# Half-height chunk transfers, weight decoding one pair sooner and two sums on GpSimd in the attention stage of a fused attention and feed-forward kernel

## The chip, the cores and the metric

One core of a Trainium2 chip runs the whole program. The metric is the time of one execution on the device in microseconds (us), the median of three runs. A profiled execution of the same program, with its own time, is the source of every row below.

The engines of the core are named as in the profile: PE is TensorE's matmul side and PEld its weight loads, DVE is VectorE, ACT is ScalarE, POOL is GpSimd, and SP is SyncE, which here only issues transfers (its queue is SPq).

## The reference

Three blocks run one after the other: a decayed linear attention over 768 tokens, 4 batches and 8 heads of 64 features, and then two feed-forward blocks over the 3072 tokens.

```python
state = zeros((B, H, D, D))
for t in range(S):
    state = gamma * state + einsum('bhd,bhe->bhde', k[:, :, t], v[:, :, t])
    y[:, :, t] = scale * einsum('bhd,bhde->bhe', q[:, :, t], state)
x = y.transpose(0, 2, 1, 3).reshape(B * S, H * D)
h = (x @ w1) * (x @ w2) @ w3          # d_ff = 1024
x = h @ w_out
h = maximum(maximum(x @ v1, x @ v2), x @ v3)   # d_ff = 768
y = h @ v_out
```

## The kernel before

**The attention stage.** The tokens of each batch are cut into chunks of 128, six to a batch, 24 in all (`CPB`, `NCH`). `seq` lists them in the order of work: batches 0 and 1 take turns for twelve chunks, then batches 2 and 3. The loop steps over pairs, `i` and `i + 1`. For a chunk the kernel computes scores (`scores`, L360), multiplies them by a mask on DVE (`attn_mask`, L365), scales v on POOL (`scale_v`, L350, with the decay factors that `decays` copies on DVE, L343), multiplies q with the running state (`attn_in`, L373), multiplies the masked scores with v (`attn_av`, L382), updates the state (`attn_st`, L393, copied by ACT, L395) and moves the result out of PSUM with its output factors on DVE (`attn_ev`, L400). Scores, masks and scaled v of the next pair are made at the end of a pair (`scores_ahead`); in the pair that ends the first two batches (`turn`, i = 10) they are made in its middle. The order of the instructions on every engine is the order of this code.

**The chunks' transfers.** A chunk is a tile of 128 partitions with four rows of 512 numbers in each: q, k, the key by token and v. `load_half` (L327) brings two of the rows, q and k or the other two, 4 KB for each partition and 512 KB in all (256 KB where a batch's last chunk needs v alone). Six chunk tiles stand in a ring (`NCK`). At the end of pair `i` the SP queue gets the four transfers of chunks `i + 6` and `i + 7`, and in the first six pairs one transfer of weights after them (`early`, L93 inside `fetch`); two more go out ahead of the loop.

**Decoding the weights.** The weights arrive as 64-bit numbers. A unit is 512 KB of them, and eight units are decoded during the attention stage. `step` alternates `decode_a` and `decode_b`. Taking in a unit (`decode_front`) is an absolute value on ACT (L124) and a clip on POOL (L126); then follow two instructions on DVE (L147, L149), a conversion on ACT (L156) and an addition on DVE (L141). `decode_b` already takes in the following unit on ACT and POOL. `plan` says at which place of which pair a step or another job is put: place 1 lies between `attn_in` and `attn_av` of the pair's first chunk, place 2 behind that chunk, and place 3 behind `scores_ahead`.

**The operands of the first feed-forward block.** Its products are formed with seven multiplications of sums in place of eight, each operand held as a high and a low part. `wgen.parts(q)` splits a weight operand into the two parts, on ACT (L211) and DVE (L212); `wgen.sums` forms sums of the raw weights on DVE (L216, L218 to L220), with `tmp`, which is `s_t`, as a buffer. `op_split` does the splitting for the activations (L254, L255), and `op_first` forms their first difference (L266). The first matmuls (L573 to L575) need the parts of operand and weight 0; the next groups need those of 1, of 2, and so on. Some of these jobs stand in `plan`, and the rest between the attention stage and the first matmul group, from L533 on, in the code's order.

Of the kernel before, what the change touches and what calls it, by code (L numbers as in the profile page):

```python
# [12 lines left out]
ALU = mybir.AluOpType  # L13
ACT = mybir.ActivationFunctionType

P = 128
# [3 lines left out]
CPB = S // C  # L20
# [27 lines left out]
def fused_kernel(ctx: ExitStack, tc: tile.TileContext, ck, w12, w3t, wo1, w123, wo2, mask, gout, gch, kdec, out):  # L48
    nc = tc.nc
# [15 lines left out]
    def spill(n, q):  # L65
        return opsp[n, q].rearrange("h p x -> p h x")

    def halves(t):
        return t.bitcast(F32).rearrange("p (h x) -> p h x", h=2)
# [135 lines left out]
    def weights(raw, n, slot=wslot, tmp=None):  # L205
        tmp = s_t[:, :n] if tmp is None else tmp
        r0, r1, r2, r3 = raw

        def parts(q):
            src, w = (r0, r1, r0, r2, tmp, r3, r1)[q], slot(q, n)  # L210
            nc.scalar.copy(out=w[:, 0], in_=src)  # L211
            nc.vector.tensor_tensor(out=w[:, 1], in0=src, in1=w[:, 0], op=ALU.subtract)  # L212

        def sums(q):
            if q == 0:
                return [lambda: nc.vector.tensor_tensor(out=tmp, in0=r2, in1=r3, op=ALU.add)]  # L216
            if q == 1:
                return [lambda: nc.vector.tensor_tensor(out=r2, in0=r2, in1=r0, op=ALU.subtract),  # L218
                        lambda: nc.vector.tensor_tensor(out=r0, in0=tmp, in1=r0, op=ALU.subtract),
                        lambda: nc.vector.tensor_tensor(out=r1, in0=r1, in1=r0, op=ALU.subtract)]  # L220
            return []

        def emit(q):
            for job in jobs(q):
                job()

        def jobs(q):
            return [lambda: parts(q)] + sums(q)

        emit.jobs, emit.parts, emit.sums = jobs, parts, sums  # L230
        return emit

    def raw_quads(n):
        return [wraw_t[0][:, i * n:(i + 1) * n] for i in range(4)]
# [14 lines left out]
    def view2(t):  # L249
        return t.rearrange("p (k n) -> p k n", k=2)  # L250

    def split_to(o, src):
        o = o.rearrange("p (h k n) -> p h k n", h=2, k=2)
        nc.scalar.copy(out=o[:, 0], in_=src)  # L254
        nc.vector.tensor_tensor(out=o[:, 1], in0=src, in1=o[:, 0], op=ALU.subtract)  # L255

    def op_split(s, src):
        split_to(op_t[s % 4][:, :], src)
# [3 lines left out]
    def t_buf(n):  # L262
        return view2(work["T"][:, :1024])

    def op_first(quad):
        nc.vector.tensor_tensor(out=quad(0, 0), in0=quad(0, 1), in1=quad(0, 0), op=ALU.subtract)  # L266

    def op_pre(n, q, quad, quiet=False):
        t, sub = t_buf(n), ALU.subtract
        if q == 2:  # L270
            op_first(quad)
            nc.vector.tensor_tensor(out=t, in0=quad(1, 1), in1=quad(0, 0), op=sub)
        elif q == 3:
            eng = nc.vector if quiet else nc.gpsimd
            eng.tensor_tensor(out=quad(0, 1), in0=quad(1, 1), in1=quad(0, 1), op=sub)
        elif q == 5:
            nc.vector.tensor_tensor(out=t, in0=t, in1=quad(1, 0), op=sub)
# [33 lines left out]
    def half(hh):  # L311
        return slice(64 * hh, 64 * hh + 64)

    seq = [(2 * g + z, j) for g in range(2) for j in range(CPB) for z in range(2)]
    last = len(seq) - 1

# [3 lines left out]
    def cks(i):  # L320
        return ck_t[i % NCK]

    def load_half(i, z):
        if i <= last:
            b, j = seq[i]
            o = 3 if z and j == CPB - 1 else 2 * z
            nc.sync.dma_start(out=cks(i)[:, o:2 * z + 2, :], in_=ck[b * CPB + j, :, o:2 * z + 2, :])  # L327

    def bank4(k, n=NP):
        return bank[k].rearrange("p (n c) -> p n c", n=n)  # L330
# [81 lines left out]
    def quad_b(n):  # L412
        return lambda k, e: xr_t[n][:, 2 * k:2 * k + 2, e, :]
# [4 lines left out]

    with tc.manual_schedule():
        load_half(0, 0)  # L420
        nc.scalar.dma_start(out=kdec_sb, in_=kdec)
        load_half(1, 0)
        nc.scalar.dma_start(out=mask_sb, in_=mask)
        load_half(0, 1)
        load_half(1, 1)
        nc.vector.memset(warm_sb, 0.0)
# [20 lines left out]
        for i in range(2):  # L447
            scores(i)
            attn_mask(i)
        wgen = weights(raw_quads(1024), 1024)  # L450
        ops_b = {}
        plan = {
            (4, 1): [step],
            (4, 3): [step],
            (6, 1): [step],
# [1 line left out]
            (8, 1): [step],  # L457
            (8, 3): [step],
            (10, 1): [step],
            (10, 3): [step],  # L460
            (12, 1): [step],
            (12, 2): [lambda: wgen.parts(0)],
            (12, 3): [step],
            (14, 1): [step],
            (14, 2): [lambda: op_split(0, quad_b(0)(0, 0))],
            (14, 3): [step],
            (16, 1): [step],
            (16, 2): [lambda: wgen.parts(1)],
            (16, 3): [step],
            (18, 1): [step],  # L470
            (18, 2): [lambda: op_first(quad_b(0))],
            (18, 3): [step],
            (20, 1): [step],
            (20, 2): [wgen.sums(0)[0]],
            (20, 3): [wgen.sums(1)[0]],
        }

        def place(i, z):
# [52 lines left out]
        rwa = b_pl.tile([P, 2048], F32, name="rwa")  # L531
        b_pl.tile([P, 24], F32, name="pad_b")
        op_split(1, quad_b(0)(1, 0))  # L533
        wgen.sums(1)[1]()
        wgen.parts(2)
        nc.vector.tensor_tensor(out=t_buf(0), in0=quad_b(0)(1, 1), in1=quad_b(0)(0, 0), op=ALU.subtract)
        op_split(2, t_buf(0))
        for t in range(3):
            nc.sync.dma_start(out=spill(0, t), in_=halves(op_t[t]))
        op_pre(0, 3, quad_b(0), quiet=True)  # L540
# [9 lines left out]
        wgen = weights(raw_quads(1024), 1024)  # L550
        for g in range(KF // GA):
            for n in range(NB):
                blk = g * NB + n
                sets = sets_b(blk)
                for q in range(7):
# [13 lines left out]
                    for p in range(GA):  # L569
# [32 lines left out]
                        z = p if blk > NB else 2 * q + p // 2  # L602
# [3 lines left out]
                    z = s - 7 * (NB - 1) - LAG  # L606
# [118 lines left out]
        wgen = weights(raw_quads(256 * GH), 256 * GH)  # L725
        GEN = (15, 18, 21, 24, 27, 30, 33, 36)
        XL = 0
        for s in range(XS):
            n, r = divmod(s, 14)
            q, kk = divmod(r, 2)  # L730
# [10 lines left out]
            for m in range(2):  # L741
                ps = bank[(4 if n % 2 == 0 else 0) + (2 if which == "b" else 0) + m]
                o = slice(m * P, (m + 1) * P)
# [77 lines left out]
        for j in range(GH):  # L821
# [14 lines left out]
            wgen = weights(raw_quads(256 * GH), 256 * GH)  # L836
# [91 lines left out]
        for s in range(7 * NB):  # L928
            n, q = divmod(s, 7)
# [9 lines left out]
            for r in range(2):  # L939
                ps = o_sets[n % 2][which][r]  # L940
                o = slice(r * P, (r + 1) * P)
# [87 lines left out]
```

## Time and profile before

| | |
|---|---|
| median of three runs | 819.75 us (819.7 to 819.98) |
| the profiled execution: time | 818.71 us |
| the profiled execution: span from first to last instruction | 816.4 us |
| outside the span | 2.31 us |
| busy: PE, DVE, ACT, POOL | 805.8, 631.4, 388.2, 74.6 us |
| granted clock of TensorE | 0.999 |
| first matmul of the feed-forward block | 82.8 us after the start |

The span runs from the first instruction to the last. The attention stage fills its first tenth. Busy time of an engine says how long it worked, not that its work decided the end; which wait ends last is read from the chain of waits and from the timeline.

### The profile page before, as it was taken

Reading aid. Unit: us, or ns where it says so; the run is one execution under the profiler, and the core shown is the slowest. Engines: PE = TensorE matmul, PEld = TensorE weight load, DVE = VectorE, ACT = ScalarE, POOL = GpSimd, SP = SyncE. Lnnn points to the kernel's source line nnn. Section 1 sums busy time; section 2 is a strip of 40 time slices with the busy share of each in tenths; the row PEclk is TensorE's granted clock in tenths of the full one; section 3 lists DMA queues with packets and bytes.
Section 4 is the critical chain, followed back from the end, with each engine's and each line's share of the span. In section 5 each row is a group of like instructions: output and inputs, shape, how many; then the busy total and the mean of one; then the engine's idle time right before and its main releaser. Section 6 shows DMA issues by size and latency. Waiting matters only on the chain.

```text
span 816.4 us, 12177 instructions
## 1 busy us (share of the span) xinstructions
PE 805.8 (99%) x4648; PEld 672.6 (82%) x4648; DVE 631.4 (77%) x795; ACT 388.2 (48%) x589; POOL 74.6 (9%) x93
## 2 busy tenths in 40 slices
PE   8999999999999999999999999999999999999998
PEld 8888888888888888888888888888888888888886
DVE  3799898989598988779799839994565565688793
ACT  2442545463336454557577545453334334434642
POOL 2443000000011111001010000000000000000000
PEclk9999999999999999999999999999999999999999
DMA  9997598789999984686789798989998699956522
GB/s 346 406 408 309 212 363 342 294 336 327 371 334 416 361 327 181 217 305 214 266 300 364 260 345 308 365 297 406 409 324 304 239 336 352 321 214 216 205 104 78
DMA packets 69961, 246.55 MB, mean 302 GB/s; under 512 B 6416, under 2 KB 6544, under 8 KB 69904
## 3 DMA queue, kind: packets, MB, share of 16 engines
q1 hardware_dynamic: 48672, 165.97, 53.8%
q10 hardware_dynamic: 21232, 79.81, 27.2%
q8 instruction: 37, 0.61, 0.3%
q14 instruction: 20, 0.16, 0.0%
HBM read 163.97 MB, written 81.79 MB: 301 GB/s over the span
## 4 chain that ended last, share of the span: by engine, by line
PE 93%; DVE 0%; issue 0%; ACT 0%; ACTq 0%
PE bank L872 11%; PE bank L873 10%; PE bank L874 10%; PE bank L575 9%; PE bank L574 9%; PE bank L573 9%; PE bank L746 5%; PE bank L747 5%; PE bank L748 5%; PE bank L944 4%; PE bank L945 4%; PE bank L943 3%; PE bank L662 2%; PE bank L661 2%; PE bank L663 2%; PE abank L382 1%
## 5 line engine op out<-in xcount | busy, mean ns | idle before, releaser
L573 PE MATMUL bank<-op,w 128*128 128x512 f32 x336 | 130.8, 389 | 0.0
L575 PE MATMUL bank<-op,w 128*128 128x512 f32 x336 | 130.7, 389 | 0.0
L574 PE MATMUL bank<-op,w 128*128 128x512 f32 x336 | 130.7, 389 | 0.0
L872 PE MATMUL bank<-op,w 128*128 128x512 f32 x330 | 128.5, 389 | 0.0
L874 PE MATMUL bank<-op,w 128*128 128x512 f32 x330 | 128.4, 389 | 0.0
L873 PE MATMUL bank<-op,w 128*128 128x512 f32 x330 | 128.4, 389 | 0.0
L126 POOL TENSOR_SCALAR dec<-dec 128x512 f32<-128x512 f32 x64 | 46.6, 729 | 554.4 <-ACT dec L124 520.5
L573 PEld LDWEIGHTS bank<-op,w 128*128 128x128 f32 x336 | 63.1, 188 | 13.3 <-issue 0.2
L574 PEld LDWEIGHTS bank<-op,w 128*128 128x128 f32 x336 | 63.1, 188 | 13.2
L575 PEld LDWEIGHTS bank<-op,w 128*128 128x128 f32 x336 | 63.1, 188 | 12.9
L872 PEld LDWEIGHTS bank<-op,w 128*128 128x128 f32 x330 | 61.9, 188 | 13.5 <-ACT bank L877 0.5
L874 PEld LDWEIGHTS bank<-op,w 128*128 128x128 f32 x330 | 61.9, 188 | 13.0
L873 PEld LDWEIGHTS bank<-op,w 128*128 128x128 f32 x330 | 61.9, 188 | 12.6
L748 PE MATMUL bank<-op,w 128*128 128x512 f32 x168 | 65.4, 389 | 0.0
L746 PE MATMUL bank<-op,w 128*128 128x512 f32 x168 | 65.4, 389 | 0.0
L747 PE MATMUL bank<-op,w 128*128 128x512 f32 x168 | 65.4, 389 | 0.0
L156 ACT ACTIVATE dec<-stg 128x512 int32<-128x512 uint32 x49 | 33.1, 676 | 52.2 <-DVE stg L149 45.8
L147 DVE TENSOR_SCALAR dec<-dec 128x512 int32<-128x512 int32 x64 | 27.0, 422 | 22.7 <-POOL dec L126 22.7
L124 ACT ACTIVATE dec<-stg 128x512 f32<-128x512 f32 x49 | 32.6, 664 | 12.7 <-DMA stg<-in_w_dram 6.5
L885 DVE TENSOR_TENSOR m<-m,bank 128x512 f32<-128x512 f32 x34 | 23.3, 684 | 19.5 <-PE bank L874 18.9
L944 PE MATMUL bank<-w,wo 128*128 128x512 f32 x96 | 37.4, 390 | 0.0
L945 PE MATMUL bank<-w,wo 128*128 128x512 f32 x96 | 37.4, 389 | 0.0
(216 smaller groups left out, 1581.7 us busy)
## 6 DMA issues: line engine op xcount, KB each, us to landing
op<-opsp ACTq DMA_DIRECT2D x53, 1024.0 KB, 8.1
opsp<-op SPq DMA_DIRECT2D x34, 1024.0 KB, 5.7
ck<-in_ck_dram SPq DMA_DIRECT2D x44, 512.0 KB, 10.1
fsp<-C SPq DMA_DIRECT2D x24, 512.0 KB, 4.8
op<-opsp SPq DMA_DIRECT2D x10, 1024.0 KB, 6.0
hsp<-m SPq DMA_DIRECT2D x32, 256.0 KB, 6.0
stg<-in_w_dram SPq DMA_DIRECT2D x15, 512.0 KB, 9.3
U<-fsp SPq DMA_DIRECT2D x14, 512.0 KB, 5.9
```

Of the source, the lines that this page charges most:

```text
L126: nc.gpsimd.tensor_scalar(out=df, in0=df, scalar1=MAX_HI, scalar2=MIN_HI, op0=ALU.min, op1=ALU.max)
L573: nc.tensor.matmul(ps, wh, x[:, 0, k, :], start=first and k == 0 and not seeded, stop=False, skip_group_check=True)
L574: nc.tensor.matmul(ps, wh, x[:, 1, k, :], start=False, stop=False, skip_group_check=True)
L575: nc.tensor.matmul(ps, wl, x[:, 0, k, :], start=False, stop=k == 1, skip_group_check=True)
L746: nc.tensor.matmul(ps, wh, x[:, 0, k, :], start=first and kk == 0 and k == 0, stop=False, skip_group_check=True)
L747: nc.tensor.matmul(ps, wh, x[:, 1, k, :], start=False, stop=False, skip_group_check=True)
L748: nc.tensor.matmul(ps, wl, x[:, 0, k, :], start=False, stop=kk == 1 and k == 1, skip_group_check=True)
L872: nc.tensor.matmul(ps, wh, x[:, 0, k, :], start=first and k == 0 and not seeded, stop=False, skip_group_check=True)
L873: nc.tensor.matmul(ps, wh, x[:, 1, k, :], start=False, stop=False, skip_group_check=True)
L874: nc.tensor.matmul(ps, wl, x[:, 0, k, :], start=False, stop=k == 1, skip_group_check=True)
L944: nc.tensor.matmul(ps, wh[:, k, o], xl[:, k], start=False, stop=False, skip_group_check=True)
L945: nc.tensor.matmul(ps, wl[:, k, o], xh[:, k], start=False, stop=k == 2, skip_group_check=True)
```

## The change

From the nineteenth chunk on (`i >= HALVES`, 18) each transfer of `load_half` becomes two, one for partitions 0 to 63 and one for 64 to 127. The decode steps begin in pair 2 in place of pair 4 and keep their order; the same 17 steps are placed, so that the last one stands in pair 18. `parts(0)` moves from pair 12 to pair 10, `parts(1)` from pair 16 to pair 18. `op_first` and the first of the weight sums go to GpSimd, at the end of pairs 16 and 18. The second sum stands in the middle of pair 20, the third one, until now behind the loop, in pair 22. Behind the loop `parts(2)` is placed after the second activation split.

```diff
-        def sums(q):
+        def sums(q, eng=nc.vector):
             if q == 0:
-                return [lambda: nc.vector.tensor_tensor(out=tmp, in0=r2, in1=r3, op=ALU.add)]
+                return [lambda: eng.tensor_tensor(out=tmp, in0=r2, in1=r3, op=ALU.add)]
...
-    def op_first(quad):
-        nc.vector.tensor_tensor(out=quad(0, 0), in0=quad(0, 1), in1=quad(0, 0), op=ALU.subtract)
+    def op_first(quad, eng=nc.vector):
+        eng.tensor_tensor(out=quad(0, 0), in0=quad(0, 1), in1=quad(0, 0), op=ALU.subtract)
...
+    HALVES = 18
...
-            nc.sync.dma_start(out=cks(i)[:, o:2 * z + 2, :], in_=ck[b * CPB + j, :, o:2 * z + 2, :])
+            n = P if i < HALVES else P // 2
+            for r in range(0, P, n):
+                nc.sync.dma_start(out=cks(i)[r:r + n, o:2 * z + 2, :], in_=ck[b * CPB + j, r:r + n, o:2 * z + 2, :])
...
         plan = {
+            (2, 1): [step],
+            (2, 3): [step],
             (4, 1): [step],
...
             (10, 1): [step],
+            (10, 2): [lambda: wgen.parts(0)],
             (10, 3): [step],
             (12, 1): [step],
-            (12, 2): [lambda: wgen.parts(0)],
             (12, 3): [step],
             (14, 1): [step],
             (14, 2): [lambda: op_split(0, quad_b(0)(0, 0))],
             (14, 3): [step],
             (16, 1): [step],
-            (16, 2): [lambda: wgen.parts(1)],
-            (16, 3): [step],
+            (16, 3): [step, lambda: op_first(quad_b(0), nc.gpsimd)],
             (18, 1): [step],
-            (18, 2): [lambda: op_first(quad_b(0))],
-            (18, 3): [step],
-            (20, 1): [step],
-            (20, 2): [wgen.sums(0)[0]],
-            (20, 3): [wgen.sums(1)[0]],
+            (18, 2): [lambda: wgen.parts(1)],
+            (18, 3): [lambda: wgen.sums(0, nc.gpsimd)[0]()],
+            (20, 2): [wgen.sums(1)[0]],
+            (22, 1): [wgen.sums(1)[1]],
         }
...
         op_split(1, quad_b(0)(1, 0))
-        wgen.sums(1)[1]()
-        wgen.parts(2)
         nc.vector.tensor_tensor(out=t_buf(0), in0=quad_b(0)(1, 1), in1=quad_b(0)(0, 0), op=ALU.subtract)
         op_split(2, t_buf(0))
+        wgen.parts(2)
```

## Rows read from the trace of the kernel before

**Rows 1.** Chain that ended last, 50 to 83 us: start, length, what
```profile
53.66 1.09 PE abank L373 x28
...
57.64 1.64 PE pair L360 x25
59.28 0.43 issue
...
60.43 1.03 PE abank L373 x32
...
65.82 0.37 issue
...
72.19 0.47 issue
...
78.78 0.23 issue
...
80.98 1.90 PE abank L382 x32
82.88 0.43 PE bank L573
```

**Rows 2.** Stretches: length, busy PE, PEld, DVE, ACT, POOL (instructions), clock, DMA share, GB/s
```profile
60.00:70.00 10.00, 9.63 (x212) 8.79 (x212) 9.82 (x14) 3.23 (x6) 4.85 (x6) 1.00 1.03 407
...
82.80:816.40 733.60, 729.95 (x3218) 603.15 (x3216) 567.85 (x706) 360.49 (x528) 44.13 (x57) 1.00 0.80 295
```

**Rows 3.** Timeline of PE, chunks 12 to 15: start, length, instruction, wait before
```profile
43.87 1.16 PE L360 MATMUL pair<-ck 64*128 64x128 f32 x16 [0.38 <-DMA ck<-in_ck_dram]
45.24 1.16 PE L360 MATMUL pair<-ck 64*128 64x128 f32 x16 [0.21 <-DMA ck<-in_ck_dram]
...
51.05 2.06 PE L360 MATMUL pair<-ck 64*128 64x128 f32 x32
```

**Rows 4.** Timeline of PE and DVE around the first decode step, pair 4
```profile
21.27 1.10 PE L373 MATMUL abank<-ck,st 64*64 64x128 f32 x32
...
24.74 0.43 DVE L147 TENSOR_SCALAR dec<-dec 128x512 int32<-128x512 int32 x1 [1.90 <-POOL dec L126]
...
25.80 2.26 PE L360 MATMUL pair<-ck 64*128 64x128 f32 x32
25.87 0.68 DVE L400 TENSOR_TENSOR xr<-abank,gout 128x512 f32<-128x512 f32 x1
...
27.14 2.35 DVE L365 TENSOR_TENSOR a<-pair,mask 128x1024 f32<-128x1024 f32 x2
```

**Rows 5.** Single transfers, by line: issue time and time to landing
```profile
L93 SPq DMA_DIRECT2D xr<-in_w_dram x1: 328/328/328, 10.9 to 10.9; - x1
...
DMA to landing us min/median/max: 9.6/9.6/9.6
...
L93 SPq DMA_DIRECT2D s_t<-in_w_dram x1: 328/328/328, 51.5 to 51.5; - x1
...
DMA to landing us min/median/max: 10.2/10.2/10.2
...
L327 SPq DMA_DIRECT2D ck<-in_ck_dram x1: 328/328/328, 66.8 to 66.8; - x1
...
DMA to landing us min/median/max: 10.0/10.0/10.0
```

**Rows 6.** Groups by line: count, busy us, mean ns, idle time before
```profile
L275 POOL TENSOR_TENSOR x<-x 128x1024 f32<-128x1024 f32 x1 | 2.4, 2413 | 0.0
...
L126 POOL TENSOR_SCALAR dec<-dec 128x512 f32<-128x512 f32 x10 | 6.1, 612 | 28.5 <-ACT dec L124 28.5
...
L124 ACT ACTIVATE dec<-xr 128x512 f32<-128x512 f32 x4 | 2.7, 676 | 0.0
```

**Rows 7.** Timeline of POOL and DVE, pairs 18 and 20
```profile
72.40 2.04 POOL L350 TENSOR_TENSOR ck<-ck,kd 128x512 f32<-128x512 f32 x2 [3.77 <-DVE kd L343]
...
76.32 1.22 DVE L216 TENSOR_TENSOR s_t<-wraw 128x1024 f32<-128x1024 f32 x1
```

## The prediction

> **What bounds the kernel now.** I read the busy times by stretch first. From 82.8 us on PE is busy for 729.95 of 733.6 us [rows 2]: behind the first feed-forward matmul the kernel is one row of matmuls, and a change in the attention stage can only move the moment at which that row begins. Before it, in the stretch from 60 to 70 us, three things are full at once: PE 9.63 us of 10, DVE 9.82 of 10, and the transfers at 407 GB/s [rows 2]. Shares can't say which of the three sets the pace, so I went to the chain that ended last. From 53.66 us to the first feed-forward matmul at 82.88 us it holds PE alone, broken by four pieces called "issue", of 0.43, 0.37, 0.47 and 0.23 us, together 1.50 us [rows 1]. So DVE, though full, is not what ends last there: PE waits for no DVE, POOL or DMA row in these 29 us. The reader is to see that a fuller engine can be the one with room.
>
> The third view, the timeline of PE a little earlier, shows where PE last waited for data: the scores of chunks 12 and 13 begin at 43.87 and 45.24 us, both when a transfer lands [rows 3]. Up to there the transfers set the pace; the change doesn't alter what is loaded before that or in which order. The floor for any gain follows: with chunk 13 landing when it does, PE can save what it idles between 45.24 and 82.88 us, and no more.
>
> **Beginning the decode one pair sooner.** The first unit of weights is issued at 10.9 us and lands 9.6 us later, at 20.5 us [rows 5]. Its step now stands in pair 2, ahead of that pair's evictions, so ACT and DVE, which work in order, stop there until it lands. ACT's absolute value (0.68), POOL's clip (0.61) [rows 6] and a tenth for the hand-overs bring it to 21.9 us; the two DVE instructions take 1.13 (from 24.74 to 25.87), then the two evictions and the copy 1.27 (25.87 to 27.14) [rows 4], which ends at 24.3. Queued behind them are the state copies on ACT, and on PE `attn_in` of pair 4, whose banks these evictions free: it began at 21.27 [rows 4] and would begin near 24.5. From the start of `attn_in` to the next scores PE needs 3.98 when nothing makes it wait (53.66 to 57.64 [rows 1]), so the scores of pair 6 move from 25.80 [rows 4] to about 28.6, a slip of 2.8 us.
>
> It isn't kept. A pair of PE's own work is that 3.98 and 2.06 for the scores [rows 3], at most 6.0 us, while the pairs up to the turn came as their chunks landed, more slowly than that. From 28.6 the scores of pair 8 follow at 34.6, of pair 10 at 40.6; add the scores, `attn_in` and `attn_av` of chunk 10 (2.06, 1.1 and 0.9) and the scores of chunk 12 (1.0), and those of chunk 13 come at 45.7 against the 45.24 that the landing allows [rows 3]. With the cadence at which PE runs without waits a little under these busy times, the slip left there is 0 to 0.5 us; I take 0.2. The cover is the waiting for transfers in pairs 4 to 10; without it the whole 2.8 us would stay. The SP queue keeps its pace: with eight transfers in flight (below) its next issue waits for a landing, not for PE.
>
> From here the steps run one pair ahead, each unit now asked for about when it lands. The last one, issued at 51.5, lands at 61.7 us [rows 5], is clipped at 63.1, about when DVE comes to it after the masks of pair 14. Such waits take DVE time which is no longer used up by the moved jobs. I count nothing.
>
> **The moved splits and sums.** `parts(0)`, one DVE split of 1.14, now precedes the masks of chunks 12 and 13 and delays the products of chunk 12 by about 0.5 us; in return it no longer stands before the eviction of chunk 13, which PE waited for until 53.66 [rows 1], 0.55 us after the scores that begin at 51.05 [rows 3] have gone through. The two cancel: `attn_in` of pair 14 begins at 53.5 to 54.0. In pairs 14 to 22 every DVE job removed is time off an engine that PE doesn't wait for [rows 1]: gain nothing.
>
> On POOL a subtraction of this size took 2.41 us [rows 6], against 1.22 on DVE [rows 7]; that price is this trace's own, so both ends are close to it. `op_first` runs behind the scaling of v in pair 16 and is done before POOL's next work at 72.40 [rows 7]. The first sum starts behind that work, at 74.4 to 74.9, and ends at 76.9 to 77.3. DVE, which did this sum at 76.32 itself [rows 7], now waits for it and does the second one at that point, to 78.5; the two masks of the last pair then end at 81.5 to 81.9. PE needs the later one for the product of chunk 23, half way through the 1.90 us that begin at 80.98, so at about 81.9 [rows 1]. Covered, by 0 to 0.4 us. If the sum came 0.5 us later, PE would lose up to 0.5.
>
> Behind the loop DVE is rid of one sum, and `parts(2)` comes last. Its matmuls are the third group: 24 matmuls at 0.227 (729.95 over 3218 [rows 2]) are 5.4 us a group, so it is needed at about 93.8 us, and five DVE jobs of 1.2 with two ACT casts between them are done before 91. Nothing.
>
> **Transfers of 64 partitions.** No row shows one. The stream in question runs from 61.7 us, where the last weights land, to 76.8, where the last chunk lands (issued at 66.8, 10.0 later [rows 5]): 15.1 us. From one side: a transfer of 512 KB takes 1.28 us of the stream at 407 GB/s, and 10.2 us from issue to landing [rows 5] are eight of them in flight; with pieces half as large eight still hold 5 us of work, so the stream need not run dry, and the time stays. From the other: if a half-height transfer takes as long as a whole one did, the stream takes 30.2 us. What PE can bear: the last chunk's v has to be scaled (half of 2.04 [rows 7]) and multiplied (0.95), so a landing at 76.8 allows an end at 79; it can come 3.9 us later before it moves the end by itself. So the stream may be slower by a quarter at no cost. Between the ends I take the rate as kept, since the rows nearest to it are those of a stream that is never empty, and both halves follow each other in one queue. Smaller pieces may also shorten the "issue" waits of PE that fall in this stream (last rival): I count 0.4 us of the 1.07 that their last three rows hold [rows 1].
>
> The Trainium skill speaks against it: "SBUF — State Buffer", section "Door 1: The DMA port swizzle", says that partitions 0 to 63 reach only half of the 16 ports that a transfer over all 128 reaches, and its next section that two transfers on the two halves serialize. No row here shows either. By the rule the stream would take twice as long, and the sum would come to 831 us in place of 819.5; that is the first rival.
>
> **Sum.** Early slip 0 to 0.5, taken as 0.2; the moved `parts(0)` 0 to 0.5 less 0 to 0.55 that PE no longer waits, taken as -0.05; late sum 0 to 0.5, taken as 0; "issue" pieces -1.07 to 0, taken as -0.4; the stream at its old rate 0. Together -1.6 to +1.5, taken as -0.25 us. On the profiled execution's own 818.71 us that is 818.5; its median stands 1.04 us above it, so 819.5 us.
>
> **The rivals.**
> - *The halves move at half the rate* (slower). Chunk 23 lands at 61.7 + 30.2 = 91.9; scaling and product add 2.2; the feed-forward block begins at 94.1 in place of 82.9, 11.2 us later: 831 us. For it: nothing here has tried such a transfer, and the stream is full. Against it: the halves that follow each other in a long queue may overlap, which no row excludes. It decides once the stream is slowed by more than a third: at one and a half times the length chunk 23 lands at 84.4 and the time is 823.4 us.
> - *The early wait isn't made good* (slower): the 2.8 us of pair 6 stay, 822.5 us. Against it: the landing rows of chunks 12 and 13 [rows 3].
> - *The "issue" pieces go* (faster). The first stretches the scores of pair 14 from 2.06 [rows 3] to 2.79 us (57.64 to 60.43 [rows 1]). If they come from instructions that have to be loaded past the chunks' transfers, smaller pieces could let them through sooner. The last three add up to 1.07 us, and to 1.8 at the first one's proportion (0.73 for 0.43): 818.0 to 818.7, and 817.4 with the 0.55 above as well. Against it: the last one, at 78.78, falls after the last landing.
>
> **How the numbers follow.** About 0.2% (1.6 us) is what a measurement of this kernel can tell from no change: 818.1 to 821.4 us. Forecast (the order changes and PE's chain stays whole, so the moved DVE work buys nothing): 0.57, with 818.3 to 821.2 as its own range. "Issue" pieces go and the time falls below 818.1: 0.13. Halves somewhat slower, 821.4 to 826: 0.12. Halves near half rate, 826 to 831: 0.14. Early wait kept: 0.04. That is faster 0.13, same 0.57, slower 0.30. The range of 8 in 10 runs from 817.6 to 825.5, which leaves out most of the half-rate case and the edge of the fast one.
>
> **What the changed profile would show.** Right: the first feed-forward matmul between 82.2 and 83.5 us; PE's `attn_in` of pair 4 near 24.5 us, with DVE's first decode instruction waiting some 5 us for POOL; chunk 13's scores still at about 45.3; a POOL subtraction of 2.4 us in pairs 16 and 18; PE alone on the chain from about 54 us. Wrong: a rate well under 400 GB/s between 62 and 77 us, and PE or POOL waiting for chunk transfers after 62 us; a wait of PE for a mask in the last pair; no "issue" pieces after 64 us.

## The result and the profile after

The changed kernel takes 827.01 us (median of five runs, 825.88 to 832.34) against 819.75 us before: a ratio of 1.0103, 95% interval 1.0082 to 1.0124. The change costs about 1%, some 7 to 8 us. The profiled execution is the longest of the five, 832.34 us with a span of 830.0 us. It holds a stretch near 300 us, long after the attention stage, where one transfer keeps PE waiting and the granted clock is 0.83 over 10 us; the other four executions lie between 825.88 and 827.10 us, so I don't count that stretch to the effect.

Line numbers of the attention stage stand four higher than in the kernel before. The busy times by stretch, with the columns of [rows 2], show the place of the loss:

```profile
20.00:30.00 10.00, 7.23 (x120) 6.65 (x118) 7.05 (x13) 4.10 (x10) 3.78 (x5) 0.83 1.03 409
...
60.00:70.00 10.00, 9.26 (x186) 8.43 (x182) 8.59 (x13) 2.63 (x5) 2.76 (x4) 1.00 1.03 242
70.00:80.00 10.00, 6.85 (x138) 5.86 (x128) 7.63 (x8) 1.69 (x3) 4.66 (x4) 1.00 1.03 251
80.00:90.00 10.00, 8.29 (x156) 7.33 (x158) 5.60 (x7) 1.75 (x3) 6.09 (x5) 1.00 0.60 204
```

From 60 to 80 us the stream of half-height transfers runs at 242 and 251 GB/s, where the whole ones ran at 407 [rows 2]. The DMA share is 1.03 in both kernels: the sixteen DMA engines count as full, and move 1.6 times less. In the 14 us from 62 to 76 us the kernel before had these totals (packets, MB, rate; then of the queue of these transfers, packets, MB, share of 16 engines):

```profile
DMA packets 1670, 5.63 MB, mean 402 GB/s; under 512 B 176, under 2 KB 176, under 8 KB 1668
...
q1 hardware_dynamic: 1668, 5.60, 100.7%
```

and the changed one these:

```profile
DMA packets 1055, 3.48 MB, mean 249 GB/s; under 512 B 212, under 2 KB 212, under 8 KB 1052
...
q1 hardware_dynamic: 1052, 3.44, 101.5%
```

The packets are as large on average (3.3 KB), but there are fewer of them in the same engine time, so each takes 1.6 times as long. That is why the share alone couldn't have shown it.

The timeline of PE in the same stretch (columns as in [rows 3]) shows who waits for it:

```profile
59.36 2.06 PE L364 MATMUL pair<-ck 64*128 64x128 f32 x32
...
67.69 0.60 PE L364 MATMUL pair<-ck 64*128 64x128 f32 x5 [0.55 <-DMA ck<-in_ck_dram]
...
71.00 1.09 PE L386 MATMUL abank<-a,ck 128*64 128x128 f32 x16 [0.76 <-POOL ck L354]
...
77.45 1.16 PE L364 MATMUL pair<-ck 64*128 64x128 f32 x14 [1.51 <-DMA ck<-in_ck_dram]
...
80.74 1.09 PE L386 MATMUL abank<-a,ck 128*64 128x128 f32 x16 [1.11 <-POOL ck L354]
...
82.80 1.09 PE L386 MATMUL abank<-a,ck 128*64 128x128 f32 x16 [0.50 <-POOL ck L354]
...
87.14 1.09 PE L377 MATMUL abank<-ck,st 64*64 64x128 f32 x28 [0.43 <-DVE xr L404]
...
90.38 0.50 PE L576 MATMUL bank<-op,w 128*128 128x512 f32 x1
```

Before, nothing but PE and four "issue" pieces stood on the chain here [rows 1]. Now PE waits for the scores' rows of a chunk (L364), and then for POOL's scaling of v (L354). The list of waits from 53 to 110 us (total, times, longest) says what POOL itself waited for:

```profile
POOL ck L354 <- DMA ck<-in_ck_dram: 11.2, 4, 4.9
...
PE pair L364 <- DMA ck<-in_ck_dram: 2.1, 2, 1.5
```

So both kinds of wait come from the transfers. The first feed-forward matmul begins at 90.38 us in place of 82.88 [rows 1], 7.5 us later; the medians differ by 7.3 us.

### The profile page after: what moved, and what is told of

The parts are those of the page before. It is cut to its first block, busy times and chain, and to the rows that moved or that the text cites. A ratio compares the mean times of both kernels' runs of the same rounds, so it can differ in the third digit from the quotient of the medians.

```text
span 830.0 us, 12214 instructions
## 1 busy us (share of the span) xinstructions
PE 810.5 (98%) x4648; PEld 675.6 (81%) x4648; DVE 630.6 (76%) x793; ACT 389.5 (47%) x589; POOL 78.3 (9%) x95
## 4 chain that ended last, share of the span: by engine, by line
PE 62%; DMA 1%; ACT 0%; issue 0%; ACTq 0%; DVE 0%
PE bank L875 10%; PE bank L876 10%; PE bank L877 10%; PE bank L751 5%; PE bank L750 5%; PE bank L749 5%; PE bank L947 3%; PE bank L946 3%; PE bank L948 3%; PE bank L666 2%; PE bank L664 2%; PE bank L665 2%; DMA op<-opsp 1%; PE bank L576 1%; PE bank L577 1%; PE bank L578 1%
## 5 line engine op out<-in xcount | busy, mean ns | idle before, releaser
L147 DVE TENSOR_SCALAR dec<-dec 128x512 int32<-128x512 int32 x64 | 27.0, 422 | 26.0 <-POOL dec L126 26.0
```

## The experiments

All ratios are to the kernel before, run on the same chip beside the experiment; "block" is the start of the first feed-forward matmul in the profiled execution.

| kernel | median us (before) | ratio, 95% interval | GB/s, 60:70 and 70:80 | block at |
|---|---|---|---|---|
| change without half-height transfers | 820.18 (818.77) | 1.0015 (1.0006 to 1.0024) | 406, 278 | 83.72 |
| half-height transfers alone | 826.25 (818.77) | 1.0087 (1.0069 to 1.0105) | 258, 262 | 88.43 |
| as many pieces, cut by rows | 820.23 (818.77) | 1.0013 (0.9996 to 1.003) | 367, 317 | 83.31 |
| both lower halves first | 828.62, one run | | 225, 236 | 90.33 |
| tall halves of 512 KB | 829.64 (819.11) | 1.0134 (1.0121 to 1.0147) | 217, 217 | 95.43 |
| halves on two queues | 829.4, one run | | 255, 265 | 93.12 |
| quarters of 128 KB | 834.57, one run | | 204, 198 | 95.78 |
| halves for the last two chunks alone | 819.75 (819.11) | 1.001 (1.0001 to 1.0019) | 402, 274 | 86.21 |
| early decoding alone | 819.45 (819.11) | 1.0002 (0.9992 to 1.0012) | 407, 274 | 82.47 |
| two sums on GpSimd alone | 819.34 (819.11) | 1.0007 (0.9998 to 1.0015) | 406, 271 | 83.43 |
| without halves, first step later | 819.45 (818.93) | 1.0011 (1.0002 to 1.002) | | 83.21 |
| without halves, sums on DVE | 819.46 (818.93) | 1.0006 (0.9996 to 1.0016) | | 84.30 |

A second figure of 271 to 317 GB/s is no lower rate: in those kernels the stream ends before 80 us, and the figure holds its pause. (With halves for the last two chunks alone it also mixes both kinds of transfer.)

**Undo the halves.** The change with its transfers left whole:

```diff
-    HALVES = 18
+    HALVES = 24
```

> The whole change except the half-height transfers (all chunks in transfers of 128 partitions). Theory H (the half-height transfers cost it all: 255 GB/s in place of 407): the stream is back at 400 GB/s or more, PE's first feed-forward matmul at 82.4 to 84.2 us, time 819 to 821 us. Rival W (the wait of the first decode step in pair 2, with the lower clock behind it, costs it, and the slow transfers only fill time that was lost already): the block still begins at 86 us or later, time 823 us or more.

Measured: 1.0015, and the stream at 406 GB/s. About 0.9 of the 1.03% is gone. What is left is small but above zero; the last four experiments are about it.

**The halves alone**, in the kernel before:

```diff
-            nc.sync.dma_start(out=cks(i)[:, o:2 * z + 2, :], in_=ck[b * CPB + j, :, o:2 * z + 2, :])
+            n = P if i < 18 else P // 2
+            for r in range(0, P, n):
+                nc.sync.dma_start(out=cks(i)[r:r + n, o:2 * z + 2, :], in_=ck[b * CPB + j, r:r + n, o:2 * z + 2, :])
```

> The kernel before with the half-height transfers alone. Theory H: 245 to 260 GB/s between 62 and 85 us, the block begins at 89 to 91 us, time 825 to 828 us. Rival W: 819.5 to 821 us.

Measured: 1.0087, with stretches like those of the changed kernel:

```profile
60.00:70.00 10.00, 8.59 (x167) 7.34 (x164) 9.07 (x12) 2.90 (x5) 3.40 (x4) 1.00 1.03 258
70.00:80.00 10.00, 6.91 (x134) 6.16 (x136) 7.88 (x10) 1.33 (x3) 3.04 (x4) 1.00 1.01 262
```

Both ways round the cause is the halves: 0.87% with them alone, 0.15% without them, together about the 1.03%. In the traces the block comes 5.55 us later with the halves alone and 0.84 us later without them; of the 7.5 us of the change, 1.1 us belong to neither alone (see the sums on GpSimd in the next section).

**Is it the number and size of the pieces, or the 64 partitions?** The kernel before, with each late transfer cut in two along its rows, so that as many pieces of the same 256 KB still span 128 partitions:

```diff
-            nc.sync.dma_start(out=cks(i)[:, o:2 * z + 2, :], in_=ck[b * CPB + j, :, o:2 * z + 2, :])
+            m = 2 * z + 2
+            cols = [(o, m, 0, 512)] if i < 18 else [(o, o + 1, 0, 512), (o + 1, m, 0, 512)] if m - o == 2 else [(o, m, 0, 256), (o, m, 256, 512)]
+            for x, y, c, d in cols:
+                nc.sync.dma_start(out=cks(i)[:, x:y, c:d], in_=ck[b * CPB + j, :, x:y, c:d])
```

> The kernel before with the same transfers cut into as many and as small pieces (256 KB, in the last two chunks' v 128 KB), but along the rows: each piece holds all 128 partitions and half of their bytes. Theory H, in the form that the 64 partitions are what costs: 395 GB/s or more, time 818.5 to 820.5 us. Rival S (small pieces or their number cost): about 250 GB/s and 825 us or more.

Measured: 1.0013 with an interval that holds 1, and

```profile
60.00:70.00 10.00, 10.00 (x220) 9.20 (x219) 9.82 (x14) 3.23 (x6) 4.80 (x6) 1.00 1.02 367
```

Small pieces cost a tenth of the rate, which the slack bears; they don't cost the 36 to 41% that the halves do.

The control from the other side keeps the number and the 512 KB of the transfers of before, and lets each take 64 partitions with all four rows in place of 128 with two (chunks 18 to 21; the last two stay whole):

```diff
-            nc.sync.dma_start(out=cks(i)[:, o:2 * z + 2, :], in_=ck[b * CPB + j, :, o:2 * z + 2, :])
+            if i < 18 or j == CPB - 1:
+                nc.sync.dma_start(out=cks(i)[:, o:2 * z + 2, :], in_=ck[b * CPB + j, :, o:2 * z + 2, :])
+            else:
+                nc.sync.dma_start(out=cks(i)[64 * z:64 * z + 64], in_=ck[b * CPB + j, 64 * z:64 * z + 64])
```

> The kernel before, its transfers of the late chunks cut the other way: each still moves 512 KB and there are as many of them, but one takes 64 partitions with all four rows of the pair in place of 128 partitions with two (the last chunk of each group stays as it was). If it is the 64 partitions that cost: 200 to 260 GB/s between 60 and 80 us, the feed-forward block begins 4 us or more later than at 82.9 us, ratio 1.005 or more. If it is the smaller size or the larger number of pieces: about 400 GB/s as before, ratio 0.999 to 1.001.

Measured: 1.0134, the slowest of the timed kernels:

```profile
60.00:70.00 10.00, 4.63 (x99) 4.01 (x98) 6.61 (x9) 2.92 (x5) 2.60 (x3) 0.88 1.02 217
70.00:80.00 10.00, 8.09 (x128) 7.25 (x128) 6.19 (x9) 1.31 (x3) 2.67 (x3) 0.78 1.01 217
```

Neither number nor size differs from before here, and the rate falls to 217 GB/s. It is the 64 partitions. (Its time also holds a later order, since q and k of a chunk are complete only with its second piece, and a granted clock of 0.66 to 0.88 between 60 and 90 us. So its ratio is no price of the rate alone.)

**Why 1.6 times and not twice?** If neighbours on opposite halves overlap a little, the order must matter. First the two lower halves of a pair of transfers, then the two upper ones:

```diff
...
-            load_half(i + NCK, 0)
-            load_half(i + NCK + 1, 0)
-            load_half(i + NCK, 1)
-            load_half(i + NCK + 1, 1)
+            for z in range(2):
+                for low in (None,) if i + NCK < 18 else (0, 64):
+                    load_half(i + NCK, z, low)
+                    load_half(i + NCK + 1, z, low)
```

> The kernel before with the half-height transfers, the order changed: the lower halves of both chunks of a pair first, then the upper halves, so that two transfers in a row go to the same 64 partitions. If the rate of 255 GB/s comes of two halves that overlap a little at their borders, longer runs on one half bring it down towards 204 GB/s and the block begins at 92 us or later, time 828 us or more. If a half-height transfer has its rate by itself, whatever its neighbour is, the rate stays at 245 to 260 GB/s and the time at 825 to 828 us.

Measured:

```profile
60.00:70.00 10.00, 7.14 (x124) 6.47 (x123) 7.01 (x10) 2.92 (x5) 2.74 (x3) 0.85 1.03 225
70.00:80.00 10.00, 9.83 (x174) 8.85 (x170) 7.91 (x10) 1.33 (x3) 3.07 (x3) 0.81 1.04 236
```

The rate falls with the length of the run on one side: 242 to 262 GB/s where the side changes after every 256 KB, 225 to 236 after two such pieces, and 217 with the tall halves. Those come in the order of `load_half`, the same side of two chunks and then the other, so their run is 1 MB. Half of 407 is 203.5. At that rate runs of 256 KB, 512 KB and 1 MB would take 1.29, 2.58 and 5.15 us; at 260, 230 and 217 GB/s they took 1.01, 2.28 and 4.83 us. That is 0.28, 0.30 and 0.32 us less (0.22 at the changed kernel's 247), so one overlap of nearly fixed length at each change of side accounts for all of them; this is an estimate from the mean rates.

The packets of the trace show it too. With each packet's bytes spread over the time that it took, the rate of the halves alone swings between 62 and 76 us from about 205 to 240 GB/s up to about 290 to 320 and back, once in every 1.0 us, which is the time of one 256 KB piece. With the tall halves it stays at about 200 to 237 for nearly all of that time, with the whole transfers of before at about 380 to 418. Two tries to make more of the overlap follow. The upper halves from ACT's queue:

```diff
...
-                nc.sync.dma_start(
+                (nc.scalar if r else nc.sync).dma_start(
...
```

> The kernel before with half-height transfers, the lower halves issued by SP and the upper halves by ACT, so that both halves stand in queues of their own. If 255 GB/s come from one queue working off one half after the other, the rate between 62 and 75 us comes back to 370 GB/s or more and the block begins before 86 us (if the waits that ACT's issues bring don't use it up). If any mixture of half-height transfers is slow, the rate stays at 240 to 270 GB/s and the block begins at 88 to 91 us.

Measured: 255 and 265 GB/s, no more than in one queue. The block came later still (93.12 us): in the list of waits from 53 to 95 us ACT's copies of the state wait 18.4 us behind its transfers. Which of PE's waits follow from that isn't shown. And halves cut once more along the rows, 128 KB each:

```diff
-            nc.sync.dma_start(out=cks(i)[:, o:2 * z + 2, :], in_=ck[b * CPB + j, :, o:2 * z + 2, :])
+            m = 2 * z + 2
+            cols = [(o, o + 1, 0, 512), (o + 1, m, 0, 512)] if m - o == 2 else [(o, m, 0, 256), (o, m, 256, 512)]
+            for x, y, c, d in cols if i >= 18 else [(o, m, 0, 512)]:
+                n = P if i < 18 else P // 2
+                for r in range(0, P, n):
+                    nc.sync.dma_start(out=cks(i)[r:r + n, x:y, c:d], in_=ck[b * CPB + j, r:r + n, x:y, c:d])
```

> The kernel before with each half-height transfer cut once more along its rows: 128 KB pieces, lower and upper 64 partitions in turn, so that runs on one half are half as long. If neighbouring halves overlap at their borders, by a fixed length, more borders give more: the rate rises from 258 to 290 GB/s or more. If a 64-partition transfer is slow by itself, it stays at 245 to 265 GB/s; if the size of the pieces counts, or their number in flight (1 MB in place of 2), it falls below 240.

```profile
60.00:70.00 10.00, 7.78 (x161) 6.88 (x160) 9.10 (x12) 2.94 (x5) 3.35 (x4) 1.00 0.74 204
70.00:80.00 10.00, 6.66 (x128) 5.93 (x128) 5.58 (x8) 1.32 (x3) 2.22 (x3) 1.00 0.60 198
```

Here the share drops to 0.74 and 0.60: the stream runs dry between pieces. So this run says nothing about the overlap; it shows that pieces of 128 KB no longer keep the stream full. The prediction had said of pieces half as large only that they would, and at 256 KB they did.

**How much slack is there?** Halves for chunks 22 and 23 alone:

```diff
-            nc.sync.dma_start(out=cks(i)[:, o:2 * z + 2, :], in_=ck[b * CPB + j, :, o:2 * z + 2, :])
+            n = P if i < 22 else P // 2
+            for r in range(0, P, n):
+                nc.sync.dma_start(out=cks(i)[r:r + n, o:2 * z + 2, :], in_=ck[b * CPB + j, r:r + n, o:2 * z + 2, :])
```

> The kernel before with transfers of 64 partitions for the last two chunks alone, 1.5 MB in place of 3.3. At the rate that such transfers had in the change's trace (250 GB/s in place of 407) the stream of these chunks takes 6.1 us in place of 3.85, so the last lands 2.3 us later. The prediction gave the last landing 3.9 us of room: by that, no loss, ratio 0.9995 to 1.001. Rival: the room is less than 2.3 us, since the mask and the product of the last pair follow the landing more closely than was reckoned: ratio 1.001 to 1.003, with a wait of PE or POOL for the last chunk.

Measured: 1.001, on the border between the two expectations. Its profiled execution is the longest of its eleven (823.27 us), and its block begins 3.3 us late. What is long in it, by the timeline of PE, is a piece called "issue":

```profile
75.11 1.65 PE L362 MATMUL pair<-ck 64*128 64x128 f32 x11 [3.01 <-issue]
```

The last landing had the room that the prediction gave it: POOL's scaling for the last pair, at 82.07 us, waits for the decay factors on DVE and for no transfer. The long piece has to do with another queue. The trace holds packets of 16 KB on a DMA queue that it calls "instruction", and each "issue" piece before scores, 23 in the traces of this case, ends 1.3 to 1.6 us after such a packet has moved. In the kernel before these packets end at 58.30, 64.85, 71.13 and 77.58 us, and PE goes on at 59.72, 66.19, 72.67 and 79.01. Here the third one begins at 72.31 us in place of 70.06 and ends at 73.63, and PE goes on at 75.11. So these pieces are, by all the rows show, waits for instructions, and here the instructions come late, while the stream beside them runs at 242 GB/s (70 to 72 us). That the halves hold them up is likely but not shown: the trace of the row pieces has a late one too (71.00 to 72.05 us, with a piece of 1.90 us behind it). Whether the 0.1% comes from such pieces stays open.

**What is left without the halves.** The early decoding alone, in the kernel before:

```diff
+            (2, 1): [step],
+            (2, 3): [step],
             (4, 1): [step],
...
-            (18, 3): [step],
-            (20, 1): [step],
```

> The kernel before with the weight decoding begun one pair sooner, and nothing else. If the early wait is what is left of the change's loss beside the transfers: PE waits for ACT some 2.5 us before pair 4, the scores of pair 14 come 1 to 3 us later than in the kernel before, ratio 1.0005 to 1.002. If the wait is made good by the landings of chunks 12 and 13, as the prediction had it: scores of chunk 13 within 0.5 us of 45.24 us, ratio 0.999 to 1.0005.

Measured: 1.0002. The wait is there and is paid back late, by the timeline of PE:

```profile
23.51 0.44 PE L373 MATMUL abank<-ck,st 64*64 64x128 f32 x4 [2.51 <-ACT dec L156]
...
29.57 2.06 PE L360 MATMUL pair<-ck 64*128 64x128 f32 x32
...
45.49 2.06 PE L360 MATMUL pair<-ck 64*128 64x128 f32 x32
...
52.19 2.06 PE L360 MATMUL pair<-ck 64*128 64x128 f32 x32
...
82.47 0.50 PE L573 MATMUL bank<-op,w 128*128 128x512 f32 x1
```

The scores of pair 6 come 3.8 us late, those of pair 14 still 1.1 us [rows 3, 4], and the block 0.4 us early [rows 1]. From the scores of pair 14 to the block it is 30.28 us in place of 31.83: 1.55 less, and the "issue" pieces, 1.50 us before [rows 1], are gone from this timeline. The 16 KB packets of the instruction queue begin 0.9 to 1.3 us sooner here than before (55.93, 62.63, 69.17 and 75.20 us in place of 57.22, 63.77, 70.06 and 76.51), and PE comes to these places later. Why the packets are sooner no run shows. So neither expectation was right as a whole: in this execution the landings of chunks 12 and 13 take up only part of the slip, and the absent "issue" pieces make good the rest.

The two sums on GpSimd alone:

```diff
...
-            (16, 3): [step],
+            (16, 3): [step, lambda: op_first(quad_b(0), nc.gpsimd)],
...
-            (18, 2): [lambda: op_first(quad_b(0))],
-            (20, 2): [wgen.sums(0)[0]],
+            (20, 2): [lambda: wgen.sums(0, nc.gpsimd)[0]()],
```

> The kernel before with the two sums on GpSimd, and nothing else. By the prediction they cost nothing: ratio 0.9995 to 1.0005. Rival: a DVE instruction beside GpSimd's 2.4 us is held until that is done, as seen with the change without its half-height transfers, and PE then waits for an eviction: a DVE instruction of 0.7 us takes 2 us or more, the block begins 0.5 to 1 us later, ratio 1.0005 to 1.0015.

Measured: 1.0007, with an interval that holds 1, and a block that begins 0.55 us later. The held DVE instruction that the rival named is there, by the timeline:

```profile
68.60 2.86 POOL L266 TENSOR_TENSOR xr<-xr 128x1024 f32<-128x1024 f32 x1
69.16 2.59 DVE L147 TENSOR_SCALAR dec<-dec 128x512 int32<-128x512 int32 x1
...
73.48 1.56 PE L373 MATMUL abank<-ck,st 64*64 64x128 f32 x32
```

L147 takes 0.43 us elsewhere [rows 4]. It ends 0.29 us after POOL does. The evictions behind it come late, and PE's `attn_in` of pair 20, which needs them, takes 1.56 us where it took 1.10 before: 0.46 of the 0.55 us. So the trace shows the rival's mechanism, and its price is too small for the ratio to tell from nothing.

In the change without halves the two meet. One variant put the first step behind the evictions of pair 2,

```diff
-            (2, 1): [step],
-            (2, 3): [step],
+            (2, 3): [step, step],
```

> The change without half-height transfers, with the first two decode steps both at the end of pair 2, so that no eviction of pair 2 stands behind the first unit's landing; every later step stands where the change has it. Theory W (the remaining 0.15% come from the early wait): the attn_in of pair 4 begins at 21 to 22 us again, the feed-forward block at 82.5 to 83.2, ratio 0.999 to 1.0005. Rival C (they come from the two sums on GpSimd, which hold a DVE instruction for as long as they run, 2.60 us in place of 0.69 in the run without halves): the block begins at 83.5 us or later, ratio 1.001 to 1.002.

and moved the wait on by one pair only, with 1.0011:

```profile
29.55 0.43 PE L377 MATMUL abank<-ck,st 64*64 64x128 f32 x4 [1.85 <-ACT dec L156]
```

The other kept the two sums on DVE at the same places:

```diff
-            (16, 3): [step, lambda: op_first(quad_b(0), nc.gpsimd)],
+            (16, 3): [step, lambda: op_first(quad_b(0))],
-            (18, 3): [lambda: wgen.sums(0, nc.gpsimd)[0]()],
+            (18, 3): [lambda: wgen.sums(0)[0]()],
```

> The change without half-height transfers, with the two sums left on DVE at the same places. Theory W: nothing gained, the block begins at 83.5 us or later, ratio 1.001 to 1.002. Rival C: PE no longer waits for an eviction before attn_in of pair 20, the block begins at 82.5 to 83.2 us, ratio 0.9995 to 1.0005. If both cost, each of the two runs gets back a part.

Measured: 1.0006, with an interval that holds 1 (one of the eleven executions, 4643.88 us, is far off, unexplained and not in the ratio). The intervals of these variants overlap, so none is shown to be better than another, and none beats the kernel before.

## Why the prediction was wrong

The forecast was 819.5 us, with 817.6 to 825.5 as the range; 827.01 lies above it.

- **The step that failed** is "Between the ends I take the rate as kept, since the rows nearest to it are those of a stream that is never empty". That the stream isn't empty was right: in the changed kernel the pieces land 9.3 us after issue, which at 249 GB/s is about nine in flight, and the DMA share stays at 1.03. It doesn't follow that the rate stays. A full queue says that the engines always have work, not how fast they do that kind of work; no row of before held a transfer of 64 partitions, and the choice between the ends had no row on its side. Measured, the stream is 407/250 = 1.6 times as long, between the forecast's 1 and the rival's 2. The kernels with halves alone, with row pieces and with tall halves show that the 64 partitions are the cause.
- **The first rival was right in its direction, and its formula only in part.** At the measured rate 61.7 + 15.1 x 1.63 gives 86.3 us for the last landing, and the last transfer, issued at 81.6 us, did land 4.7 us later, at 86.3. But the block doesn't hang on that landing. The 2.2 us behind it would put the block at 88.5, and it began at 90.38; that the halves alone began theirs at 88.43 is chance, since the formula at their own 260 GB/s gives 87.5. PE's last wait for the stream is the one at 82.80 us for chunk 21's scaled v (82.02 with the halves alone), and from there PE works through to the block, with one wait of 0.43 us for an eviction. The place of the waits was as the prediction's signs named: the scores and POOL's scaling, after 62 us. The chance was put wrongly: 0.26 for anything slower than 821.4 us by this cause.
- **The early wait.** PE's `attn_in` of pair 4 begins at 24.03 us (forecast "near 24.5"), behind a decode instruction that waits 5.53 us for POOL (forecast "some 5"). The slip at the scores of pair 6, forecast as 2.8 us, was 3.8 us with the early decoding alone and 4.5 in the changed kernel. Its timeline of PE shows why:

```profile
24.03 0.43 PE L377 MATMUL abank<-ck,st 64*64 64x128 f32 x4 [2.53 <-ACT dec L156]
24.71 1.09 PE L377 MATMUL abank<-ck,st 64*64 64x128 f32 x28 [0.24 <-DVE xr L404]
25.79 1.92 PE L386 MATMUL abank<-a,ck 128*64 128x128 f32 x16
...
30.26 2.06 PE L364 MATMUL pair<-ck 64*128 64x128 f32 x32
...
45.99 2.06 PE L364 MATMUL pair<-ck 64*128 64x128 f32 x32
```

Behind the wait 16 matmuls of `attn_av` take 1.92 us, where 1.09 is usual, in a stretch whose mean granted clock is 0.83. The prediction priced the wait and not slower matmuls behind it. Chunk 13's scores come 1.03 us into the row at 45.99, so at 47.0 where about 45.3 was forecast; of the slip 1.8 us are left here and 1.3 with the early decoding alone, against the forecast's 0 to 0.5. But the clock doesn't always fall. In the change without halves PE has the same wait, the granted clock over 20 to 30 us is 1.00, and by its timeline the forecast holds:

```profile
23.58 0.44 PE L377 MATMUL abank<-ck,st 64*64 64x128 f32 x4 [2.51 <-ACT dec L156]
...
28.17 2.06 PE L364 MATMUL pair<-ck 64*128 64x128 f32 x32
...
44.50 2.06 PE L364 MATMUL pair<-ck 64*128 64x128 f32 x32
```

There the slip at pair 6 is 2.4 us, and chunk 13's scores come at 45.5, 0.3 us later than the 45.24 of before. So the cover by the landings was right as a mechanism, and the term was mis-sized where the clock fell. The early decoding alone cost nothing measurable in the end (1.0002).
- **The "issue" pieces.** The term of -0.4 us didn't come. Its premise, that these are waits for instructions, is borne out (see the halves for the last two chunks); that smaller pieces let the instructions through sooner is not. With the halves alone the scores of pair 18 begin where they did before (64.29 us, 64.22 before), and the 16 KB packet in their time begins at 65.28 us in place of 63.77.
- **The sums on GpSimd.** The price was right, 2.36 to 2.38 us against 2.41 (2.86 once, in the sums alone). That an engine PE doesn't wait for has room wasn't the whole of it: a DVE instruction beside the POOL one is held. In the change without halves, by the timeline, PE meets this:

```profile
68.20 2.38 POOL L266 TENSOR_TENSOR xr<-xr 128x1024 f32<-128x1024 f32 x1
68.54 2.60 DVE L141 CUSTOM_DVE_ANT_0 wraw<-s_t,dec 128x1024 uint16<-128x1024 uint16 x1
...
73.69 1.09 PE L377 MATMUL abank<-ck,st 64*64 64x128 f32 x28 [0.67 <-DVE xr L404]
...
79.92 0.38 PE L364 MATMUL pair<-ck 64*128 64x128 f32 x2 [0.93 <-issue]
```

L141, 0.68 us elsewhere, takes 2.60, the evictions behind it come late, and PE waits for one. This and the early slip are candidates for the 0.15% that stay without halves (+0.02% and +0.07% when alone, each within its uncertainty). The moved splits and weight sums are a third, which no run tried alone: the same timeline has a wait of 0.54 us for an eviction at 60.84 us, ahead of both GpSimd sums. The split between them isn't settled. In the changed kernel the slow stream also makes the second GpSimd sum late, by the timeline:

```profile
82.70 2.36 POOL L216 TENSOR_TENSOR s_t<-wraw 128x1024 f32<-128x1024 f32 x1
85.09 1.23 DVE L218 TENSOR_TENSOR wraw<-wraw 128x1024 f32<-128x1024 f32 x1 [2.52 <-POOL s_t L216]
86.31 0.68 DVE L404 TENSOR_TENSOR xr<-abank,gout 128x512 f32<-128x512 f32 x1
```

The sum stands behind a scaling that waited for its transfer, DVE waits for the sum, and the eviction and masks behind it come late. From PE's last wait for the stream to the block it is 7.58 us here and 6.41 with the halves alone, 1.2 us more: the prediction's term for a late sum, 0 to 0.5, taken as 0, was too small once the stream was slow.

The Trainium skill, which the prediction set beside its sum, pointed the right way. Its page "SBUF — State Buffer", section "Door 1: The DMA port swizzle", gives about 218 GB/s as the limit of 64 partitions; the tall halves ran at 217. The section "Can I just issue two DMAs to hit both halves?" of that page says that two such transfers serialize, at 6% over a single one; in the full stream here alternating halves ran at 242 to 262 GB/s, 19 to 29% over 203.5, and the measurement decides.

## What to carry to other kernels

In a stream that fills its queue, cut a transfer along its rows and not across the partitions: 256 KB pieces over 128 partitions kept 367 GB/s, pieces of the same size over 64 had 242 to 262. Read the rate beside the DMA share, because the share stays at 1.03 while the rate falls by 40%; and where no row shows the new kind of transfer, a queue that is never empty is no ground for choosing the good end. A wait put ahead of PE cost more than its length where the matmuls behind it ran at a lower clock, and less where PE would have stood still later anyway, so price both.

## What was unexpected of the hardware

- The rate of half-height transfers depends on their order: 242 to 262 GB/s when the halves alternate after 256 KB, 225 to 236 after 512 KB, 217 when 1 MB of one half follows in a row.
- After PE's wait at 21 to 24 us the granted clock over 20 to 30 us was 0.83, against 1.00 before; as matmuls run at one of two levels, 1.2 or 2.4 GHz, this is a part of the stretch at the lower one. In the change without halves it was 1.00 behind a wait of the same length.
- A DVE instruction issued during a POOL instruction of 2.4 to 2.9 us was held until shortly after its end: L141 2.60 us in place of 0.68, L147 2.59 in place of 0.43. The Trainium skill ("SBUF — State Buffer", section "Who interferes with whom") says that one of the two blocks fully while they share a port, and these rows agree.
- PE's "issue" pieces stand before the same last 9, 11 and 13 matmuls of the scores in several kernels, with lengths from 0.2 to 3.01 us, and each ended 1.3 to 1.6 us after a 16 KB packet of the instruction queue had moved. One such packet that began 2.25 us later than before went with the piece of 3.01 us.
